# Expert visits of 384 rows, a one-instruction maximum and column sums that move: a change to a filter, routing and feed-forward kernel

## The chip, the core and the metric

The kernel runs on one core of a Trainium2 chip. A core has a matrix engine (TensorE; PE in the profile, with its weight loads as PEld), a vector engine (VectorE, DVE), an activation engine (ScalarE, ACT), a general engine (GpSimd, POOL), and a queue engine that issues most transfers (SyncE, SP). Each engine works through its own list of instructions in order; they wait for one another by semaphores. The metric is the time of one execution on the device in microseconds (us), lower is better.

## The reference

Eight sequences of 3072 tokens with 256 channels pass through three layers. `N` is 8 x 3072 = 24576 tokens.

```
X = rfft(x, axis=1);  y = irfft(X * (filt_r + 1j*filt_i))          # a long convolution, per channel
xn, en = y / |y|, emb / |emb|
logits = xn @ en.T / tau;  e = argmax(logits);  gate = softmax(logits)[e]
y[e] = gate * (relu(y @ w1[e]) @ w2[e])                           # 8 experts, 256 -> 1024 -> 256
h = y @ w_in;  out = (h - tanh(h)) @ w_out                        # 256 -> 2048 -> 256
```

Every matrix product of the last two layers is taken as three products: each operand is split into a high part that the fast matrix format holds exactly and a low rest, and high x high, high x low and low x high are summed.

## The kernel before, in words

The program has three stages that overlap at their ends. In the first, `fft_phase`, the filter is done as matrix products with transfers through device memory between the steps; the router scores each token, and each token's row (256 values, gate and token number) is scattered into a `region` in device memory with one segment of `CAP` rows for each expert, filled from its start.

In the second, class `Moe`, a *visit* takes 256 consecutive rows (`TV`) of one segment through its expert's two layers. There are 103 visits (`NV`): the first nine (`KV`) take rows of the fullest expert among the early batches and run beside the end of the first stage; the other 94 follow a schedule that `moe_schedule` works out on the device, with up to seven spare visits, since each expert's last visit can be part empty. A visit has four steps `b2`, and step by step the generator `visits` (its loop is at the end of the function) issues in this order:

- `up(v, b2)`: 12 matmuls into a PSUM tile `h` (two blocks of 128 hidden features, 6 matmuls each, with 256 rows as columns);
- for visit `v+1`: `split` of one quarter of the expert's weights into high and low (steps 0 and 1: `w1h` on ScalarE, `w1l` on VectorE, L752; steps 2 and 3: `w2h` on ScalarE, `w2l` on GpSimd, L752), and its rows: step 0 scales them by the gate (`ys`, GpSimd L763, and the token numbers `it`, VectorE L766), step 1 transposes them (`yt`, VectorE L771), step 2 splits them (`yh` on ScalarE L778, `yl` on VectorE L779);
- `relu(v, b2)`: `hh` on ScalarE (L801), the rest `hl` on VectorE (L802);
- for visit `v+2`: the transfer of one quarter of the weights (`wload`, skipped on the device where the expert stays the same) and, in step 2, of its rows `y` (`load`, four transfers on SP's queue);
- in step 3 (and in step 1 for the first 7 scheduled visits) one *side step*: a third of the work of converting a 128 x 256 tile of the feed-forward's 64-bit weights (`f64_split`, mostly VectorE);
- `down` of the step two before, 12 matmuls into `o`. After a visit's last `down`, `finish` copies `o` to `x2` and its absolute value to `xa` (ScalarE L823, L825), keeps a running maximum `mx` (VectorE L826), and sends `x2` off.

So TensorE's order at a boundary is `up(v,2) down(v,0) up(v,3) down(v,1) up(v+1,0)`, and the first matmuls of `up(v+1,0)` need `yl` of visit v+1. On VectorE that `yl` stands behind `mx` of visit v-1, which stands behind the last `down` of v-1.

In the third stage, `ff_phase`, 48 tiles of 512 tokens pass through the feed-forward in 16 steps each: 6 matmuls of 512 columns (L961) and 12 of 256 (L1004). Before tile 46 `limit` forms a bound from `mx` and the column sums of |w_in| (`l1`), which decides on the device whether a second, general pass is needed.

Of the kernel before, what the change touches and what calls it, by code (L numbers as in the profile page):

```python
# [27 lines left out]
S = 3072  # L28
E = 8
# [8 lines left out]
TV = 256  # L38
# [79 lines left out]
def fft_phase(tc, K, x, fr, fn, fi, emb, tau, region, base, NB, CAP, moe):  # L118
# [3 lines left out]
    with ExitStack() as es:  # L122
# [288 lines left out]
        for i in range(2 * E):  # L411
            at(31 + i, zeros, i // 2, i % 2 * 128)
# [48 lines left out]
def f64_split(nc, pool, src, hi, lo, n):  # L461

    v = nc.vector
    H, L = src[:, :, 1], src[:, :, 0]
    t = lambda nm, dt: pool.tile([128, n], dt, name=nm)
    a, m, l, f, r = t("cva", I32), t("cvm", I32), t("cvl", I32), t("cvf", F32), t("cvr", F32)
    v.tensor_scalar(a, H, 20, 0x7FF, op0=ALU.logical_shift_right, op1=ALU.bitwise_and)
    v.tensor_scalar(a, a, 896, 0, op0=ALU.subtract, op1=ALU.max)
    v.tensor_scalar(a, a, 255, None, op0=ALU.min)
    v.tensor_scalar(a, a, 23, None, op0=ALU.logical_shift_left)  # L470
    v.tensor_scalar(m, H, 31, 31, op0=ALU.logical_shift_right, op1=ALU.logical_shift_left)
    v.tensor_tensor(a, a, m, op=ALU.bitwise_or)
# [11 lines left out]
    return f  # L484


def ff_weights(tc, cp, cv, w_in, w_out):

    nc = tc.nc
    wih = cp.tile([128, 2, FF], F32R, name="wih")  # L490
    wil = cp.tile([128, 2, FF], F32R, name="wil")
    wo = cp.tile([128, 16, 2, D], F32R, name="wo")
    l1 = cp.tile([128, FF], F32R, name="l1w")
    W = 256

    def load(src):
        s = cv.tile([128, W, 2], I32, name="cvs", bufs=2)
        nc.sync.dma_start(flat(s), src.bitcast(I32))
        return s

    def step_in(s, k, q):
        c = slice(W * q, W * q + W)
        f = yield from f64_split(nc, cv, s, wih[:, k, c], wil[:, k, c], W)
        if k == 0:
            nc.scalar.activation(l1[:, c], f, AF.Abs)
        else:
            nc.scalar.activation(f, f, AF.Abs)
            nc.vector.tensor_tensor(l1[:, c], l1[:, c].bitcast(F32), f, op=ALU.add)

    def steps():  # L510
        todo = [(w_in[128 * k : 128 * k + 128, W * q : W * q + W], step_in, k, q) for k in range(2) for q in range(FF // W)]
        todo += [(w_out[128 * fb : 128 * fb + 128], lambda s, fb: f64_split(nc, cv, s, wo[:, fb, 0], wo[:, fb, 1], D), fb)
                 for fb in range(16)]
        s = load(todo[0][0])
        yield
        for i, (_, f, *args) in enumerate(todo):
            t = load(todo[i + 1][0]) if i + 1 < len(todo) else None
            yield from f(s, *args)
            yield
            s = t  # L520

    return (wih, wil, wo, l1), steps()
# [15 lines left out]
def moe_schedule(tc, cp, cnt, done, numbers, CAP, step):  # L538
# [17 lines left out]
    v.tensor_scalar(t, left, float(TV - 1), None, op0=ALU.add)  # L556
    v.tensor_copy(ti, t)
    v.tensor_scalar(ti, ti, 8, None, op0=ALU.logical_shift_right)
# [59 lines left out]
class Moe:  # L618
# [6 lines left out]
    def __init__(self, tc, gp, region, w1, w2, x2T, ids, mx, N, CAP):  # L625
        self.tc, self.gp, self.region, self.w1, self.w2 = tc, gp, region, w1, w2
        self.x2T, self.ids, self.mx, self.N, self.CAP = x2T, ids, mx, N, CAP
        self.KV = (N - 2 * S) // (8 * TV)
        self.NV = N // TV + 7
# [9 lines left out]
    def choose(self, base, first, dec):  # L639
# [68 lines left out]
    def visits(self):  # L708
# [4 lines left out]
        W, X, H, O, E = {}, {}, {}, {}, {}  # L713

        def load(v):
            y = fp.tile([128, 8, 66], F32, name="y", bufs=3)
            top = 8 * CAP - TV
            r = self.val(self.begin, 0, v, top) if v < KV else self.val(self.sc, v - KV, 0, top)
            rv = region[bass.ds(r, TV)].rearrange("(t j) (i c) -> i j t c", j=32, i=4)
            for i in range(4):  # L720
                d = nc.sync.dma_start(y[32 * i : 32 * i + 32], rv[i])
# [32 lines left out]
        f2 = lambda z: z.rearrange("p k t c -> p (k t c)")  # L754

        def rows(v):

            y, yt = X[v], None
            ys = fp.tile([128, 2, 8, 32], F32, name="ys")
            it = fp.tile([32, 32], I32, name="it", bufs=2)  # L760
            it2 = fp.tile([32, 32], I32, name="it2", bufs=3)
            def scale():
                nc.gpsimd.tensor_tensor(ys.rearrange("p k t c -> p t k c"), y[:, :, :64].rearrange("p t (k c) -> p t k c", k=2),  # L763
                                        y[:, :, 64:65].unsqueeze(3).to_broadcast([128, 8, 2, 32]), op=ALU.mult)
                nc.vector.memset(it, 0)
                nc.vector.tensor_copy(it[:, :8], y[:32, :, 65:66].bitcast(I32).rearrange("p t o -> p (t o)"))  # L766

            def turn():
                nonlocal yt
                yt = ip.tile([128, 2, 8, 32], F32, name="yt")  # L770
                nc.vector.transpose(f2(yt), f2(ys))  # L771
                nc.vector.transpose(it2, it)

            def parts():
                yh = ip.tile([128, 2, TV], F32R, name="yh")
                yl = ip.tile([128, 2, TV], F32R, name="yl")
                X[v] = (yh, yl, it2)
                nc.scalar.activation(flat(yh), f2(yt), AF.Copy)  # L778
                nc.vector.tensor_tensor(flat(yl), f2(yt), flat(yh).bitcast(F32), op=ALU.subtract)  # L779
# [3 lines left out]
        def up(v, b2):  # L783
            w1h, w1l = W[v][:2]
            yh, yl, _ = X[v]
            k = 4 * (v - KV) + b2
            h = self.hp[k // 2 % 2 if k >= 0 else 0].tile([128, 2, TV], F32, name="h")
            for j in range(2):
                c = slice(128 * (2 * b2 + j), 128 * (2 * b2 + j) + 128)
                n = 0  # L790
                for k in range(2):
                    for p, q in ((w1h, yh), (w1h, yl), (w1l, yh)):
                        nc.tensor.matmul(h[:, j], p[:, k, c], q[:, k], start=n == 0, stop=n == 5)  # L793
                        n += 1
            H[v, b2] = h

        def relu(v, b2):
            h = H[v, b2]
            hh = yp.tile([128, 2, TV], F32R, name="hh", bufs=4)
            hl = yp.tile([128, 2, TV], F32R, name="hl", bufs=4)  # L800
            nc.scalar.activation(hh, h, AF.Relu)  # L801
            nc.vector.scalar_tensor_tensor(hl, h, 0.0, hh.bitcast(F32), op0=ALU.max, op1=ALU.subtract)  # L802
            H[v, b2] = (hh, hl)

        def down(v, b2):
            w2h, w2l = W[v][2:]
            hh, hl = H.pop((v, b2))
            if b2 == 0:
                O[v] = self.op[(v - KV + 1) % 2 if v >= KV else 0].tile([128, 2, TV], F32, name="o")
            for j in range(2):  # L810
                fb = 2 * b2 + j
                for d in range(2):
                    c = slice(128 * d, 128 * d + 128)
                    for n, (p, q) in enumerate(((w2h, hh), (w2h, hl), (w2l, hh))):
                        nc.tensor.matmul(O[v][:, d], p[:, fb, c], q[:, j], start=fb == 0 and n == 0 and d == 0,  # L815
                                         stop=fb == 7 and n == 2 and d == 1)
# [244 lines left out]
def build(tc, a, out, NB):  # L1061
# [3 lines left out]
    with ExitStack() as es:  # L1065
# [4 lines left out]
        mx = gp.tile([128, 512], F32, name="mx")  # L1070
        nc.vector.memset(mx, 0.0)
# [3 lines left out]
        moe = Moe(tc, gp, region, a["w1"], a["w2"], x2T, ids, mx, N, CAP)  # L1075
        with tc.manual_schedule():
# [23 lines left out]
            ff_phase(tc, x2T, ids, out, weights, mx, N, todo[1])  # L1100
# [32 lines left out]
```

## Time and profile before

| | us |
|---|---|
| three runs | 4189.06, 4167.3, 4185.1 (median 4185.1) |
| the profiled execution | 4176.74, its span 4174.9 |
| first stage until the first visit | 583.9 |
| nine early visits, until the first scheduled one | 133.0 |
| 94 scheduled visits | 1278.1 |
| feed-forward | 2179.9 |

The stages' bounds are the starts of the first `up` matmul of visit 0, of visit 9, and of the feed-forward. In the profile each engine's busy time counts the union of its instructions; a time in brackets behind an instruction is the idle time of its engine just before it and who ended it. The granted clock is TensorE's, as a share of 2.4 GHz.

### The profile page before, as it was taken

To read this page: it belongs to the slowest core of one execution; us is meant where nothing else is said; L and a number is where in the kernel's file an instruction comes from. 1 tells how busy PE (TensorE), PEld (TensorE's weight loads), DVE (VectorE), ACT (ScalarE), POOL (GpSimd) and SP (SyncE) were. 2 spreads that over 40 slices of the span, in tenths; PEclk is the share of its full clock that TensorE was granted. 3 is DMA by queue.
4 is the path that set the end of the run, shared out by engine and by line. 5 is a ranking of instruction groups with operands and counts; after the bars stand their busy time and mean duration, and the time that the engine had idled before them with its cause. 6 is when DMAs were issued, how large, how long until landed. Compare 5 with 4: busy or idle time off the path is not lost.

```text
span 4174.9 us, 73338 instructions
## 1 busy us (share of the span) xinstructions
PE 3949.5 (95%) x25988; PEld 3562.5 (85%) x25988; DVE 2853.3 (68%) x4459; ACT 2617.5 (63%) x4385; POOL 2199.2 (53%) x1601
## 2 busy tenths in 40 slices
PE   6999889899889998899999999999999999999998
PEld 3666669899889898899999999999999999999987
DVE  4899986989889898898555555555555555555554
ACT  3555544555555555555677777777777777777765
POOL 2466664444444545455455555555555555555555
PEclk8999999999999999999999999999999999999999
DMA  9989753221221222212100000001001000000000
GB/s 270 290 275 287 248 178 88 52 65 49 67 67 48 65 60 55 67 50 60 36 25 27 21 24 29 21 24 29 21 22 30 21 21 28 25 21 28 25 16 17
DMA packets 302863, 297.67 MB, mean 71 GB/s; under 512 B 157457, under 2 KB 245402, under 8 KB 302490
## 3 DMA queue, kind: packets, MB, share of 16 engines
q1 hardware_dynamic: 280666, 238.89, 20.3%
q0 software_dynamic: 18432, 51.14, 3.4%
q8 instruction: 206, 3.38, 0.3%
q10 hardware_dynamic: 3392, 2.90, 0.2%
q14 instruction: 167, 1.37, 0.1%
HBM read 342.33 MB, written 130.72 MB: 113 GB/s over the span
## 4 chain that ended last, share of the span: by engine, by line
PE 51%; DMA 1%; ACT 0%; issue 0%; DVE 0%; POOL 0%; POOLq 0%; ACTq 0%; DVEq 0%
PE po L1004 25%; PE h L961 25%; DMA out<-ob,ix 1%; POOL gl L969 0%; ACT u L976 0%; DVE g L979 0%; DVE s L978 0%; ACT gh L968 0%; ACT s L977 0%; ACT ob L1010 0%; DVE lm L939 0%; POOL out L1013 0%; POOL allmax L944 0%; DVE big L945 0%; DVE big L946 0%
## 5 line engine op out<-in xcount | busy, mean ns | idle before, releaser
L969 POOL TENSOR_TENSOR gl<-g,gh 128x512 fp32r<-128x512 f32 x768 | 997.3, 1299 | 954.6 <-ACT gh L968 946.8
L978 DVE SCALAR_TENSOR_TENSOR s<-s,u 128x512 f32<-128x512 f32 x768 | 534.8, 696 | 936.4 <-ACT s L977 934.7
L1004 PE MATMUL po<-wo,gh 128*128 128x256 f32 x6144 | 1117.1, 280 | 0.0
L1004 PEld LDWEIGHTS po<-wo,gh 128*128 128x128 f32 x6144 | 994.6, 188 | 65.0
L1004 PE MATMUL po<-wo,gl 128*128 128x256 f32 x3072 | 864.4, 281 | 3.9 <-POOL gl L969 3.7
L976 ACT ACTIVATE u<-h 128x512 f32<-128x512 f32 x768 | 458.5, 597 | 591.1 <-PE h L961 591.0
L752 POOL TENSOR_TENSOR w2l<-raw,w2h 128x1024 fp32r<-128x1024 f32 x188 | 501.4, 2686 | 403.4 <-ACT w2h L751 403.3
L961 PE MATMUL h<-xh,wih 128*128 128x512 f32 x1536 | 615.9, 401 | 0.1
L961 PE MATMUL h<-xl,wih 128*128 128x512 f32 x1536 | 605.7, 394 | 0.0
L961 PE MATMUL h<-xh,wil 128*128 128x512 f32 x1536 | 604.4, 393 | 0.0
L979 DVE TENSOR_TENSOR g<-s,h 128x512 f32<-128x512 f32 x768 | 528.4, 688 | 85.9 <-POOL gl L969 3.7
L1004 PEld LDWEIGHTS po<-wo,gl 128*128 128x128 f32 x3072 | 579.2, 189 | 4.3 <-POOL gl L969 4.3
L793 PE MATMUL h<-yl,w1h 128*128 128x256 f32 x1648 | 486.2, 295 | 92.4 <-DVE yl L779 92.4
L977 ACT ACTIVATE s<-u,beta 128x512 f32<-128x512 f32 x768 | 556.1, 724 | 25.2
L815 PE MATMUL o<-hl,w2h 128*128 128x256 f32 x1648 | 482.5, 293 | 27.3 <-DVE hl L802 27.3
L801 ACT ACTIVATE hh<-h 128x512 fp32r<-128x512 f32 x412 | 244.9, 594 | 403.9 <-PE h L793 403.0
L968 ACT ACTIVATE gh<-g 128x512 fp32r<-128x512 f32 x768 | 486.2, 633 | 11.1 <-DVE g L979 6.1
L793 PE MATMUL h<-yh,w1h 128*128 128x256 f32 x1648 | 483.0, 293 | 4.4 <-DVE hl L802 2.8
L793 PE MATMUL h<-yh,w1l 128*128 128x256 f32 x1648 | 482.6, 293 | 2.1 <-DVE w1l L752 2.1
L815 PE MATMUL o<-hh,w2h 128*128 128x256 f32 x1648 | 481.5, 292 | 0.0
L815 PE MATMUL o<-hh,w2l 128*128 128x256 f32 x1648 | 480.0, 291 | 0.0
L793 PEld LDWEIGHTS h<-yl,w1h 128*128 128x128 f32 x1648 | 330.6, 201 | 101.6 <-DVE yl L779 100.7
(198 smaller groups left out, 7131.1 us busy)
## 6 DMA issues: line engine op xcount, KB each, us to landing
raw<-in_w SPq DMA_DIRECT2D x376, 512.0 KB
y<-region SPq DMA_DIRECT2D x412, 66.0 KB
xt<-in_x SPq DMA_DIRECT2D x48, 512.0 KB
z1d<-a SPq DMA_DIRECT2D x96, 256.0 KB
A<-z1d SPq DMA_DIRECT2D x64, 384.0 KB
z3d<-b SPq DMA_DIRECT2D x128, 192.0 KB
bt<-z3d SPq DMA_DIRECT2D x96, 256.0 KB
x2T<-x SPq DMA_DIRECT2D x94, 256.0 KB
```

The costliest lines, as they stand in the source:

```text
L752: eng.tensor_tensor(l, r, h.bitcast(F32), op=ALU.subtract)
L793: nc.tensor.matmul(h[:, j], p[:, k, c], q[:, k], start=n == 0, stop=n == 5)
L801: nc.scalar.activation(hh, h, AF.Relu)
L815: nc.tensor.matmul(O[v][:, d], p[:, fb, c], q[:, j], start=fb == 0 and n == 0 and d == 0, stop=fb == 7 and n == 2 and d == 1)
L961: nc.tensor.matmul(h, a[:, k, c], b[:, k], start=n == 0, stop=n == 5)
L968: nc.scalar.activation(gh, g, AF.Copy)
L969: nc.gpsimd.tensor_tensor(gl, g, gh.bitcast(F32), op=ALU.subtract)
L976: nc.scalar.activation(u, h, AF.Square)
L977: nc.scalar.activation(s, u, AF.Square, bias=beta)
L978: nc.vector.scalar_tensor_tensor(s, s, KAPPA, u, op0=ALU.add, op1=ALU.mult)
L979: nc.vector.tensor_tensor(g, s, h, op=ALU.mult)
L1004: nc.tensor.matmul(po[a // 2][:, a % 2], p[:, a], wo[:, f, q], start=f == 0 and n == 0 and a % 2 == 0, stop=f == 15 and n == 2 and a % 2 == 1)
```

## The change

`TV` becomes 384 for all visits but the first nine, which keep 256 (`TE`). There are then 74 visits, 65 of them scheduled, and the spare ones are of 384 rows too. Each of a visit's two feature blocks gets a PSUM bank of its own (384 of 512 columns), so `h` has four banks as before but two steps fill them instead of four; `o` gets two banks a visit, and two visits alternate over four. The ReLU and the copy to `x2` go in two instructions, one for each bank. `xa` and the running maximum go; one reduction of |x2| on VectorE writes one column of `mx` for each visit. The side step stands in step 1 too for the first 36 scheduled visits. `y` has two buffers instead of three, `hh` and `hl` three instead of four, `yt` one instead of two. The column sums of |w_in| leave the weight conversion and are formed in tile 45 of the feed-forward. The first stage clears 384 rows of each segment instead of 256 (24 transfers instead of 16), and the schedule counts visits by multiplying with 171/512 where it shifted.

```diff
-TV = 256
+TE = 256
+TV = 384
...
-        for i in range(2 * E):
-            at(31 + i, zeros, i // 2, i % 2 * 128)
+        for i in range(TV // 128 * E):
+            at(31 + i, zeros, *divmod(128 * i, TV))
...
-        f = yield from f64_split(nc, cv, s, wih[:, k, c], wil[:, k, c], W)
-        if k == 0:
-            nc.scalar.activation(l1[:, c], f, AF.Abs)
-        else:
-            nc.scalar.activation(f, f, AF.Abs)
-            nc.vector.tensor_tensor(l1[:, c], l1[:, c].bitcast(F32), f, op=ALU.add)
+        yield from f64_split(nc, cv, s, wih[:, k, c], wil[:, k, c], W)
...
-        self.NV = N // TV + 7
+        self.NV = self.KV + (N - self.KV * TE) // TV + 7
+        self.mx = gp.tile([128, self.NV], F32, name="mx")
...
-        self.op.append(self.pool("mo2", 1, space=PSUM))
+        self.op.append(self.pool("mo2", 3, space=PSUM))
...
-            y = fp.tile([128, 8, 66], F32, name="y", bufs=3)
+            y = fp.tile([128, NT, 66], F32, name="y", bufs=2)
...
-            k = 4 * (v - KV) + b2
-            h = self.hp[k // 2 % 2 if k >= 0 else 0].tile([128, 2, TV], F32, name="h")
+            if v < KV:
+                t = self.hp[0].tile([128, 2, TE], F32, name="h")
+                h = [t[:, 0], t[:, 1]]
+                H[v, b2] = [t]
+            else:
+                k = 4 * (v - KV) + b2
+                h = [self.hp[k % 2].tile([128, 512], F32, name="h")[:, :TV] for j in range(2)]
+                H[v, b2] = h
...
-            nc.scalar.activation(hh, h, AF.Relu)
-            nc.vector.scalar_tensor_tensor(hl, h, 0.0, hh.bitcast(F32), op0=ALU.max, op1=ALU.subtract)
+            for j, t in enumerate(h):
+                oh, ol = (hh, hl) if len(h) == 1 else (hh[:, j], hl[:, j])
+                nc.scalar.activation(oh, t, AF.Relu)
+                nc.vector.scalar_tensor_tensor(ol, t, 0.0, oh.bitcast(F32), op0=ALU.max, op1=ALU.subtract)
...
-            nc.scalar.activation(x2, o, AF.Copy)
-            xa = yp.tile([128, 2, TV], F32, name="xa", bufs=1)
-            nc.scalar.activation(xa, o, AF.Abs)
-            nc.vector.tensor_tensor(mx, flat(xa), mx, op=ALU.max)
+            for d in range(2):
+                nc.scalar.activation(x2[:, d], o[d], AF.Copy)
+            nc.vector.tensor_reduce(mx[:, v : v + 1], x2, axis=AX.XY, op=ALU.max, apply_absolute_value=True)
...
+        def column_sums(q):
+
+            c = slice(TM * q, TM * q + TM)
+            a = [cp.tile([128, TM], F32, name=f"abs{k}") for k in range(2)]
+            for k in range(2):
+                nc.scalar.activation(a[k], wih[:, k, c].bitcast(F32), AF.Abs)
+            nc.vector.tensor_tensor(l1[:, c], *a, op=ALU.add)
...
+                if t == NT - 3 and f % 4 == 2:
+                    column_sums(f // 4)
```

The first place is VectorE's order over one visit boundary late in the scheduled visits, where a visit has one side step (the four `cv...` rows are one). Before:

```order
L771 STREAM_TRANSPOSE yt<-ys 128x512
L772 STREAM_TRANSPOSE it_18787<-it 32x32
L802 SCALAR_TENSOR_TENSOR hl<-h,hh 128x512
L826 TENSOR_TENSOR mx<-xa,mx 128x512
L779 TENSOR_TENSOR yl<-yt,yh 128x512
L802 SCALAR_TENSOR_TENSOR hl<-h,hh 128x512 x2
L474 TENSOR_SCALAR cvm<-cvs 128x256
L475 TENSOR_SCALAR cvl<-cvs 128x256
L476 TENSOR_TENSOR cvm<-cvm,cvl 128x256
L477 TENSOR_TENSOR cvf<-cva,cvm 128x256
L752 TENSOR_TENSOR w1l<-raw_5490,w1h 128x1024
```

The same piece of a visit after the change, with its new line numbers:

```order
L778 STREAM_TRANSPOSE yt<-ys 128x768
L779 STREAM_TRANSPOSE it_17096<-it 32x32
L818 SCALAR_TENSOR_TENSOR hl<-h,hh 128x384 x2
L846 TENSOR_REDUCE mx<-x_17163 128x1
L786 TENSOR_TENSOR yl<-yt,yh 128x768
L818 SCALAR_TENSOR_TENSOR hl<-h,hh 128x384 x4
L476 TENSOR_SCALAR cvm<-cvs 128x256
L477 TENSOR_SCALAR cvl<-cvs 128x256
L478 TENSOR_TENSOR cvm<-cvm,cvl 128x256
L479 TENSOR_TENSOR cvf<-cva,cvm 128x256
L757 TENSOR_TENSOR w1l<-raw_5497,w1h 128x1024
```

The order of the pieces is the same; the maximum reads one operand instead of two, and each `hl` is two instructions.

The second place is the same boundary in one of the first 36 scheduled visits after the change, on VectorE:

```order
L778 STREAM_TRANSPOSE yt<-ys 128x768
L779 STREAM_TRANSPOSE it_11692<-it 32x32
L818 SCALAR_TENSOR_TENSOR hl<-h,hh 128x384 x2
L476 TENSOR_SCALAR cvm<-cvs 128x256
L477 TENSOR_SCALAR cvl<-cvs 128x256
L478 TENSOR_TENSOR cvm<-cvm,cvl 128x256
L479 TENSOR_TENSOR cvf<-cva,cvm 128x256
L846 TENSOR_REDUCE mx<-x_11763 128x1
L786 TENSOR_TENSOR yl<-yt,yh 128x768
L818 SCALAR_TENSOR_TENSOR hl<-h,hh 128x384 x4
```

A side step stands there between `hl` of step 1 and the maximum, which the visits of before have only seven times.

## Rows read from the trace of the kernel before

**Rows 1.** The page, busy time and share of the span by engine.
```profile
PE 3949.5 (95%) x25988; PEld 3562.5 (85%) x25988; DVE 2853.3 (68%) x4459; ACT 2617.5 (63%) x4385; POOL 2199.2 (53%) x1601
```

**Rows 2.** Windows: us; PE, PEld, DVE, ACT, POOL busy; granted clock, DMA share, GB/s.
```profile
0.00:583.90 583.90, 499.30 (x2120) 341.33 (x2120) 485.77 (x1037) 282.92 (x717) 326.50 (x302) 0.95 0.85 265
...
716.90:1995.00 1278.10, 1158.37 (x9049) 1148.25 (x9050) 1143.44 (x1579) 732.68 (x1077) 618.79 (x279) 0.94 0.23 59
1995.00:4174.90 2179.90, 2163.71 (x13829) 1952.10 (x13827) 1135.88 (x1595) 1537.91 (x2450) 1189.01 (x961) 1.00 0.08 24
```

**Rows 3.** Who PE waited for in the scheduled visits: us, times, longest.
```profile
PE h L793 <- DVE yl L779: 92.4, 41, 3.8
PE o L815 <- DVE hl L802: 27.3, 9, 5.2
```

**Rows 4.** Timeline of PE: start, us, instruction, idle before and its releaser.
```profile
1501.49 0.28 PE L793 MATMUL h<-yh,w1h 128*128 128x256 f32 x1
...
1507.25 0.28 PE L793 MATMUL h<-yh,w1h 128*128 128x256 f32 x1
...
1518.77 0.28 PE L793 MATMUL h<-yh,w1h 128*128 128x256 f32 x1
1521.42 0.39 PE L793 MATMUL h<-yl,w1h 128*128 128x256 f32 x1 [2.38 <-DVE yl L779]
```

**Rows 5.** Window just behind that wait, columns as in Rows 2.
```profile
1522.60:1525.50 2.90, 2.90 (x16) 2.90 (x15) 2.83 (x5) 1.55 (x2) 1.04 (x1) 0.50 0.00 0
```

**Rows 6.** Timeline of DVE over the same two visits.
```profile
1502.80 0.69 DVE L826 TENSOR_TENSOR mx<-xa,mx 128x512 f32<-128x512 f32 x1 [0.66 <-ACT xa L825]
1504.27 2.48 DVE L779 TENSOR_TENSOR yl<-yt,yh 128x512 fp32r<-128x512 f32 x1 [0.77 <-ACT yh L778]
...
1507.88 1.31 DVE L467 TENSOR_SCALAR cva<-cvs 128x256 int32<-128x256 int32 x1
...
1510.75 1.22 DVE L752 TENSOR_TENSOR w1l<-raw,w1h 128x1024 fp32r<-128x1024 f32 x1
...
1515.84 2.76 DVE L826 TENSOR_TENSOR mx<-xa,mx 128x512 f32<-128x512 f32 x1
1518.53 2.84 DVE L779 TENSOR_TENSOR yl<-yt,yh 128x512 fp32r<-128x512 f32 x1
```

**Rows 7.** Timeline of POOL over the same two visits.
```profile
1503.80 5.23 POOL L752 TENSOR_TENSOR w2l<-raw,w2h 128x1024 fp32r<-128x1024 f32 x2 [7.29 <-ACT w2h L751]
1510.93 1.95 POOL L763 TENSOR_TENSOR ys<-y 128x512 f32<-128x512 f32 x1 [1.90 <-DVE cva L472]
1515.32 5.51 POOL L752 TENSOR_TENSOR w2l<-raw,w2h 128x1024 fp32r<-128x1024 f32 x2 [2.44 <-ACT w2h L751]
```

**Rows 8.** Timeline of PE over one step of the feed-forward.
```profile
2501.15 0.40 PE L961 MATMUL h<-xh,wih 128*128 128x512 f32 x1
...
2502.56 0.40 PE L1004 MATMUL po<-wo,gh 128*128 128x256 f32 x2
...
2503.97 0.40 PE L961 MATMUL h<-xh,wih 128*128 128x512 f32 x1
```

**Rows 9.** Groups by line: shapes, count, busy us, mean ns, idle before.
```profile
L976 ACT ACTIVATE u<-h 128x512 f32<-128x512 f32 x768 | 458.5, 597 | 591.1 <-PE h L961 591.0
L802 DVE SCALAR_TENSOR_TENSOR hl<-h,hh 128x512 fp32r<-128x512 f32 x412 | 268.3, 667 | 38.0 <-ACT hh L801 37.8
L752 DVE TENSOR_TENSOR w1l<-raw,w1h 128x1024 fp32r<-128x1024 f32 x188 | 236.0, 1255 | 5.0 <-ACT w1h L751 4.9
L942 DVE TENSOR_REDUCE bound<-mx 128x1 f32<-128x512 f32 x1 | 0.7, 677 | 0.0
```

**Rows 10.** Timeline of SP's queue, the rows of a later visit.
```profile
1507.04 1.90 SPq L721 DMA_DIRECT2D y<-region  x4
```

**Rows 11.** Timelines of DVE and PE at one change of expert.
```profile
1219.21 0.16 DVE L766 COPY it<-y 32x8 int32<-32x8 int32 x1 [4.73 <-DMA y<-region]
...
1220.02 0.58 PE L815 MATMUL o<-hl,w2h 128*128 128x256 f32 x1 [4.33 <-DVE hl L802]
```

More of the change, by code (lines that the diff above doesn't have):

```diff
@@ L520, in steps @@
             s = t
-    return (wih, wil, wo, l1), steps()
+    return (wih, wil, wo), steps()
 def moe_numbers(tc, cp):
@@ L555, in moe_schedule @@
     v.tensor_tensor(left, cnt, done, op=ALU.subtract)
-    v.tensor_scalar(t, left, float(TV - 1), None, op0=ALU.add)
+    assert TV == 3 * 128 and CAP < 250 * 128
+    v.tensor_scalar(t, left, 127.0, None, op0=ALU.add)
     v.tensor_copy(ti, t)
-    v.tensor_scalar(ti, ti, 8, None, op0=ALU.logical_shift_right)
+    v.tensor_scalar(ti, ti, 7, None, op0=ALU.logical_shift_right)
+    v.tensor_copy(t, ti)
+    v.tensor_scalar(t, t, 2.0, 171.0, op0=ALU.add, op1=ALU.mult)
+    v.tensor_copy(ti, t)
+    v.tensor_scalar(ti, ti, 9, None, op0=ALU.logical_shift_right)
     nv = A("scnv")
@@ L752, in split @@
             eng.tensor_tensor(l, r, h.bitcast(F32), op=ALU.subtract)
-        f2 = lambda z: z.rearrange("p k t c -> p (k t c)")
         def rows(v):
-            y, yt = X[v], None
-            ys = fp.tile([128, 2, 8, 32], F32, name="ys")
+            n = size(v)
+            nt = n // 32
+            y, yt = X[v][:, :nt], None
+            ys = fp.tile([128, 2 * TV], F32, name="ys")[:, : 2 * n]
             it = fp.tile([32, 32], I32, name="it", bufs=2)
@@ L792, in up @@
                     for p, q in ((w1h, yh), (w1h, yl), (w1l, yh)):
[L793 removed]
+                        nc.tensor.matmul(h[j], p[:, k, c], q[:, k], start=n == 0, stop=n == 5)
                         n += 1
[L795 removed]
         def relu(v, b2):
+            n = size(v)
+            hh = yp.tile([128, 2, TV], F32R, name="hh", bufs=3)[:, :, :n]
+            hl = yp.tile([128, 2, TV], F32R, name="hl", bufs=3)[:, :, :n]
             h = H[v, b2]
[L799 to L802 removed]
+            for j, t in enumerate(h):
+                oh, ol = (hh, hl) if len(h) == 1 else (hh[:, j], hl[:, j])
+                nc.scalar.activation(oh, t, AF.Relu)
+                nc.vector.scalar_tensor_tensor(ol, t, 0.0, oh.bitcast(F32), op0=ALU.max, op1=ALU.subtract)
             H[v, b2] = (hh, hl)
@@ L808, in down @@
             if b2 == 0:
-                O[v] = self.op[(v - KV + 1) % 2 if v >= KV else 0].tile([128, 2, TV], F32, name="o")
+                if v < KV:
+                    t = self.op[0].tile([128, 512], F32, name="o")
+                    O[v] = [t[:, :TE], t[:, TE:]]
+                else:
+                    O[v] = [self.op[(2 * (v - KV) + d + 1) % 4 > 0].tile([128, 512], F32, name="o")[:, :TV] for d in range(2)]
             for j in range(2):
@@ L814, in down @@
                     for n, (p, q) in enumerate(((w2h, hh), (w2h, hl), (w2l, hh))):
-                        nc.tensor.matmul(O[v][:, d], p[:, fb, c], q[:, j], start=fb == 0 and n == 0 and d == 0,
-                                         stop=fb == 7 and n == 2 and d == 1)
+                        nc.tensor.matmul(O[v][d], p[:, fb, c], q[:, j], start=fb == 0 and n == 0 and (d == 0 or v >= KV),
+                                         stop=fb == 7 and n == 2 and (d == 1 or v >= KV))
             if b2 == 3:
@@ L914, in ff_phase @@
     nc = tc.nc
-    wih, wil, wo, l1 = weights
+    wih, wil, wo = weights
     NT = N // TM
@@ L1099, in build @@
             moe.go_on(sc, side, ahead)
-            ff_phase(tc, x2T, ids, out, weights, mx, N, todo[1])
+            ff_phase(tc, x2T, ids, out, weights, moe.mx, N, todo[1])
 def arrange(x, filt_r, filt_i, moe_expert_emb, moe_tau, moe_w1, moe_w2, moe2_w_in, moe2_w_out):
```

64 lines of the change are left out of this document (33 added, 31 removed).

## The prediction

> **What bounds the kernel now.** I read the busy shares first [rows 1]: TensorE is busy 95% of the span, so time can only come from its idle stretches, from a slow clock or from fewer columns. The windows by stage say where those are [rows 2]: in the feed-forward TensorE is busy 2163.7 of 2179.9 us at full clock, while the 94 scheduled visits last 1278.1 us with 1158.4 busy, a granted clock of 0.94, and VectorE busy 1143.4, nearly as long as TensorE. That stage is the change's place.
>
> Its floor comes from the timeline of TensorE [rows 4]: from 1501.49 to 1507.25 it does half a visit, 48 matmuls, without a gap: 5.76 us, 0.120 us for 256 columns, 11.52 us a visit, 1082.9 us for 94. So 195.2 us are lost: 119.7 idle (1278.1 - 1158.4) and 75.5 of slowed work. The second follows from the first: behind the wait that ends at 1521.42 a window has granted clock 0.50, that is 1.2 GHz of 2.4 [rows 5]. Each microsecond of waiting has therefore cost 195.2 / 119.7 = 1.63 us.
>
> The waits name two releasers [rows 3]: `yl` (92.4 us, 41 times) and `hl` (27.3 us, 9 times). To see why `yl` is late I laid the timelines of VectorE and GpSimd beside TensorE's, and count from the start of `up(v,2)`: 1501.49 in one visit, 1513.01 (11.52 later) in the next. In both GpSimd starts its two `w2l` of 2.6 us at +2.31 [rows 7]. In the first, `mx` begins at +1.31 and takes 0.69; `yl` then runs beside GpSimd, takes 2.48 and ends at +5.26, when the first `w2l` has ended [rows 6]. TensorE wants it at +5.88. In the second, `mx` begins at +2.83, behind GpSimd's start, and takes 2.76; `yl` follows and takes 2.84, until the second `w2l` has ended. TensorE wanted `yl` at 1518.89 and goes on at 1521.42, 2.53 us late. `mx` was late because VectorE worked from 1506.75 to 1515.84, 9.09 us, without a pause. A visit of 11.52 us is too short for VectorE's list plus its waits for GpSimd.
>
> **The change, part by part.** *Columns.* 94 visits of 256 become 65 of 384: 24960 columns for 24064, 3.7% more. No row shows a matmul of 384 columns. If what 0.120 us holds over 256 / 2.4 = 106.7 ns is a fixed 13.3 ns, it takes 173.3 ns; if all grows with columns, 180.0. The feed-forward's step has 6 matmuls of 512 columns in 1.41 us and 12 of 256 in 1.41 us [rows 8]: there twice the columns take twice the time, 0.235 and 0.1175, so three quarters of 0.235 is 176 ns. I take 178, between that and this stage's own rate: 17.09 us a visit, 1110.9 us for 65, with ends 1081 and 1123. Unlike the waits this part gains nothing; it costs 28 us over 1082.9.
>
> *The wait for `yl`.* `up(v+1,0)` now wants it at 8.54 + 0.18 = +8.72. GpSimd's pair does as much work for a visit as before, so its first `w2l` ends at +2.31 + 2.61 = +4.92 again. VectorE's rate is (1255 - 690) / 512 = 1.10 ns a column, from `w1l` [rows 9] and the free `mx` [rows 6]. `yl` ends at +5.26 + 256 x 1.10 ns = +5.54, 3.2 us early, if the maximum lies ahead of it. From `yl` to the next maximum VectorE had 9.09 us of work; now an `hl` of 384 columns takes 667 - 128 x 1.10 = 526 ns [rows 9], eight of them 1.54 us more than four of 667, and the transposes 0.28 more: 10.91. That ends at +16.45, before the next visit's zero, and the maximum waits for `x2` until +1.31. In the first 36 scheduled visits a second side step is added, 2.87 us (1507.88 to 1510.75, [rows 6]): VectorE is there at +2.23. The maximum itself, a reduction of 768 values, takes 677 + 256 x 1.10 = 0.96 us [rows 9] and ends at +3.19, before +4.92. So `yl` runs in the same gap in every visit, and the waiting of 92.4 us goes. Late next is nothing within 1.73 us; beyond that `yl` falls behind the second `w2l`, ends near +8.8, and with `hl` of step 2 behind it costs TensorE about 0.8 us. I take none.
>
> No row shows a reduction beside GpSimd; beside it `mx` took 0.69 to 2.76. I take 0.96, since the maximum ends before GpSimd's first instruction does in either case. The Trainium skill (SBUF — State Buffer, section SBUF: two separate sides) says that a VectorE instruction with two operands in that memory, or in a two-port mode, and a GpSimd instruction block each other for the whole instruction. The trace agrees for `mx` and `yl`; by that rule the one-operand reduction is not held, which makes the first rival below less likely.
>
> *Two-step depth of `h`.* `up(v+1,0)` needs the banks of `up(v,2)`, so `hl` of step 2. Its first half ends at +5.54 + 0.53 = +6.07, wanted at +8.54: nothing, covered by 2.5 us; without the cover, what is late adds one for one.
>
> *The rows `y`.* Four transfers of half as many bytes again, in two buffers whose readers have ended a visit before. Issued at +5.55 [rows 10], read by GpSimd 3.89 us later [rows 7]; half as long again is +11.4, and VectorE's copy of the token numbers wants them at 5.54 + 4 x 0.526 + 2.87 + 1.16 = +11.7. At a change of expert they come late behind the weights: the copy waited 4.73 us, `hl` behind it, TensorE 4.33 [rows 11]. These are the 27.3 us of [rows 3]. The time from issue to use grows by several microseconds; I keep half, 13.7 x 1.63 = 22 us, with ends 0 and 60.
>
> *Edits with small prices.* The column sums: 8 ScalarE instructions of 0.597 us [rows 9] and 4 of VectorE in the feed-forward, where ScalarE is idle 642 us and VectorE half the time [rows 2]: nothing, at most 8 us without that cover. What they replace leaves the visits, where I count it as nothing. Eight more clearing transfers, 1.08 MB at 265 GB/s in a stage with DMA share 0.85 [rows 2]: 0 to 4 us, I take 2. Four more VectorE instructions on 8 columns in the schedule: at most 4 x 0.68, I take 1. The early visits lose `xa` and `mx` beside TensorE's work: nothing.
>
> *Sum.* 1110.9 + 22 - 1278.1 + 3 = -142. On the profiled run, 4176.7 - 142 = 4034.8; the runs' median lies 8.4 above it, so 4043 us.
>
> **Rivals.** *VectorE stays the bound in the 36 visits with two side steps.* For it: it was the twin of TensorE in [rows 2], and the side steps' own waits for GpSimd may be longer than in my one sample. Against: 1.7 us of room in each visit. If every second of them loses 2.53 x 1.63 = 4.1 us: 18 x 4.1 = 74, 4117 us.
>
> *A matmul has a larger fixed part than I allow*, so that fewer, longer ones pay. If 384 columns took 162.5 ns, 65 visits would last 1014 us and the time would be 3946. Against it stands that both sizes lie above such a line: 120 and 235 ns where it gives 109 and 216. The line is the Trainium skill's (TensorE: Matmul & The Clock Gate, section Back-to-back issue gap): columns / 2.4 plus 2.5 ns. The trace does not agree.
>
> *The rows `y` come late in every visit, and the kernel is slower.* Place: VectorE's copy of token numbers, with `hl` and `w1l` queued behind it, and TensorE behind `hl`. It decides from a landing later than +13.4, some 8 us from issue, twice today's; it outweighs the gain from 142 / 65 = 2.2 us a visit. At the price of a change of expert, 65 x 4.33 x 1.63 = 459: 4502 us. Against it: 3.89 us today, and transfers take a DMA share of only 0.23.
>
> *The gain is eaten at the boundary.* With `h` two steps deep each late `hl` stops TensorE earlier than before; if a visit loses 1.34 us so, 2.2 with the clock, the time stays 4185. It needs VectorE some 4 us behind the timetable above.
>
> **How the numbers follow.** My forecast 0.76, with a range of its own of 3990 to 4095 (from 1081 without waits to 1123 with 60 us of them). The rivals 0.12, 0.04, 0.05 and 0.03. A difference of 0.5%, 21 us, is about what a measurement of this kernel can tell. Faster 0.76 + 0.12 + 0.04 = 0.92, the same 0.03, slower 0.05. The range 3985 to 4115 leaves out the rule's case, the slow one and the tie.
>
> **What would show it.** In the new profile: 65 scheduled visits, most of 16.6 to 17.3 us; matmuls of 384 columns at 173 to 180 ns; almost no wait of TensorE for `yl`; the maximum near 0.96 us; granted clock of the stage above 0.98; waits for `hl` only at changes of expert; feed-forward 2180 us. Wrong would be a stage of over 1200 us, visits that alternate between two lengths, or `it` waiting for `y` in most of them.

## The result and the profile after

The changed kernel took 4030.8 us, median of 4 executions (4024.8 to 4034.2); the kernel before 4181.0 beside it. The ratio is 0.9643, 95% interval 0.9613 to 0.9672. Measured once more on another chip (the last experiment) it is 0.9643 again. The forecast was 4043 us, with a range from 3985 to 4115.

The page of the changed kernel, the row that answers to [rows 1]:

```profile
PE 3904.8 (97%) x23204; PEld 3527.1 (88%) x23204; DVE 2621.8 (65%) x4370; ACT 2514.1 (62%) x4318; POOL 2051.7 (51%) x1514
```

The windows by stage, columns as in [rows 2], with the early visits as second row:

```profile
0.00:590.70 590.70, 501.98 (x2120) 342.19 (x2120) 485.42 (x1037) 282.76 (x717) 327.04 (x302) 0.95 0.84 264
590.70:729.65 138.95, 131.36 (x992) 122.62 (x993) 86.97 (x253) 60.18 (x142) 62.77 (x60) 0.98 0.39 112
729.65:1822.50 1092.85, 1087.21 (x6267) 1085.93 (x6266) 909.67 (x1483) 606.07 (x1004) 476.65 (x193) 1.00 0.27 70
1822.50:4023.00 2200.50, 2184.23 (x13829) 1976.39 (x13828) 1139.70 (x1599) 1565.05 (x2458) 1185.26 (x961) 1.00 0.08 24
```

The scheduled visits went from 1278.1 to 1092.85 us, at full clock, with TensorE idle for 5.6 us instead of 119.7. The other stages became longer: the first by 6.8, the early visits by 5.95 (138.95 - 133.0), the feed-forward by 20.6. Together that is -185.25 + 6.8 + 5.95 + 20.6 = -151.9, the difference of the profiled executions (4176.74 and 4024.83).

Who TensorE waited for in the scheduled visits (us, times, longest); of the two rows of [rows 3] the first has no successor:

```profile
PE h L807 <- DVE hl L818: 5.6, 4, 2.1
```

TensorE's timeline at the quarter points of one late visit:

```profile
1518.81 0.33 PE L807 MATMUL h<-yh,w1h 128*128 128x384 f32 x1
1518.98 0.33 PE L807 MATMUL h<-yl,w1h 128*128 128x384 f32 x1
...
1527.13 0.33 PE L807 MATMUL h<-yh,w1h 128*128 128x384 f32 x1
...
1535.45 0.33 PE L807 MATMUL h<-yh,w1h 128*128 128x384 f32 x1
1535.62 0.33 PE L807 MATMUL h<-yl,w1h 128*128 128x384 f32 x1
```

From 1518.81 to 1535.45 there are 96 matmuls and no gap: 16.64 us, 173.3 ns for 384 columns. 55 of the 65 visits begin 16.64 us before the next.

VectorE from `up(v,2)` (1527.13) of that visit:

```profile
1527.85 0.95 DVE L846 TENSOR_REDUCE mx<-x 128x1 f32<-128x768 f32 x1 [1.52 <-ACT x L845]
1529.54 2.53 DVE L786 TENSOR_TENSOR yl<-yt,yh 128x768 fp32r<-128x768 f32 x1 [0.73 <-ACT yh L785]
1531.99 1.68 DVE L818 SCALAR_TENSOR_TENSOR hl<-h,hh 128x384 fp32r<-128x384 f32 x3
...
1537.18 1.29 DVE L773 COPY it<-y 32x12 int32<-32x12 int32 x1
```

GpSimd beside it, answering to [rows 7]:

```profile
1528.85 5.48 POOL L757 TENSOR_TENSOR w2l<-raw,w2h 128x1024 fp32r<-128x1024 f32 x2 [6.51 <-ACT w2h L756]
1536.30 2.15 POOL L769 TENSOR_TENSOR ys<-y 128x768 f32<-128x768 f32 x1 [1.97 <-DMA y<-region]
```

Counted from 1527.13, the maximum ends at +1.67, before GpSimd begins at +1.72; `yl` ends at +4.94 and is wanted at 1535.62, +8.49: 3.55 us early. The copy `it` finds its rows at +10.05 without waiting.

### The profile page after: what moved, and what is told of

It reads as the page before. It is cut to its first block, busy times and chain, and to the rows that moved or that the text cites. A ratio compares the mean times of both kernels' runs of the same rounds, so it can differ in the third digit from the quotient of the medians.

```text
span 4023.0 us, 65752 instructions
## 1 busy us (share of the span) xinstructions
PE 3904.8 (97%) x23204; PEld 3527.1 (88%) x23204; DVE 2621.8 (65%) x4370; ACT 2514.1 (62%) x4318; POOL 2051.7 (51%) x1514
## 3 DMA queue, kind: packets, MB, share of 16 engines
q1 hardware_dynamic: 275714, 241.83, 21.3%
## 4 chain that ended last, share of the span: by engine, by line
PE 85%; DVE 7%; DMA 4%; issue 2%; POOL 1%; SPq 1%; ACT 1%; POOLq 0%; DVEq 0%; ACTq 0%
PE po L1034 27%; PE h L991 26%; PE h L807 14%; PE o L835 14%; DVE u L261 1%; DVE v L260 1%; DVE v L259 1%; DMA out<-ob,ix 1%; PE z L254 1%; PE z L269 1%; PE z L296 1%; PE L L308 1%; PE z L229 1%; DMA region<-Y,pi 1%; DMA z1d<-a 1%
## 5 line engine op out<-in xcount | busy, mean ns | idle before, releaser
L1034 PE MATMUL po<-wo,gh 128*128 128x256 f32 x6144 | 1143.0, 282 | 0.0
L1006 ACT ACTIVATE u<-h 128x512 f32<-128x512 f32 x768 | 459.0, 598 | 584.1 <-PE h L991 583.9
L757 POOL TENSOR_TENSOR w2l<-raw,w2h 128x1024 fp32r<-128x1024 f32 x130 | 349.9, 2692 | 416.7 <-ACT w2h L756 414.4
L817 ACT ACTIVATE hh<-h 128x384 fp32r<-128x384 f32 (+1 forms) x556 | 269.5, 498 | 458.1 <-PE h L807 443.4
L998 ACT ACTIVATE gh<-g 128x512 fp32r<-128x512 f32 x768 | 485.4, 632 | 11.2 <-PE po L1034 4.9
L807 PE MATMUL h<-yh,w1h 128*128 128x384 f32 (+1 forms) x1184 | 392.4, 331 | 10.7 <-DVE hl L818 7.3
L807 PE MATMUL h<-yh,w1l 128*128 128x384 f32 (+1 forms) x1184 | 389.5, 329 | 2.4 <-DVE w1l L757 2.3
L807 PE MATMUL h<-yl,w1h 128*128 128x384 f32 (+1 forms) x1184 | 389.4, 329 | 0.1
L835 PE MATMUL o<-hh,w2h 128*128 128x384 f32 (+1 forms) x1184 | 388.4, 328 | 0.2 <-ACT x L845 0.2
L835 PE MATMUL o<-hl,w2h 128*128 128x384 f32 (+1 forms) x1184 | 388.2, 328 | 0.0
L835 PE MATMUL o<-hh,w2l 128*128 128x384 f32 (+1 forms) x1184 | 388.1, 328 | 0.0
L991 PEld LDWEIGHTS h<-xh,wil 128*128 128x128 f32 x1536 | 288.5, 188 | 71.0
```

Of the source, the lines that this page charges most:

```text
L757: eng.tensor_tensor(l, r, h.bitcast(F32), op=ALU.subtract)
L807: nc.tensor.matmul(h[j], p[:, k, c], q[:, k], start=n == 0, stop=n == 5)
L817: nc.scalar.activation(oh, t, AF.Relu)
L835: nc.tensor.matmul(O[v][d], p[:, fb, c], q[:, j], start=fb == 0 and n == 0 and (d == 0 or v >= KV), stop=fb == 7 and n == 2 and (d == 1 or ...
L991: nc.tensor.matmul(h, a[:, k, c], b[:, k], start=n == 0, stop=n == 5)
L998: nc.scalar.activation(gh, g, AF.Copy)
```

## The experiments

They ran on four chips; each ratio is against the kernel before on the same chip.

**The maximum alone, with 256 rows** (the kernel before, and):

```diff
-            xa = yp.tile([128, 2, TV], F32, name="xa", bufs=1)
-            nc.scalar.activation(xa, o, AF.Abs)
-            nc.vector.tensor_tensor(mx, flat(xa), mx, op=ALU.max)
+            nc.vector.tensor_reduce(mx[:, v : v + 1], x2, axis=AX.XY, op=ALU.max, apply_absolute_value=True)
```

> The kernel before, with one part of the change: the absolute copy and the running maximum go, one reduction of |x2| takes their place; visits stay at 256 rows. Theory A (the maximum's wait for GpSimd is what makes yl late): the maximum still comes at +2.8 us but ends at +3.5, ahead of the end of GpSimd's first w2l at +4.9, so yl runs in the first gap of every visit and the visits take 11.52 us: scheduled visits 1090 to 1140 us, time 4020 to 4060. Rival B (a visit of 256 rows is too short for VectorE's list, whatever the maximum costs): visits still alternate, scheduled visits over 1200 us, time over 4105.

Measured: 4048.4 us, ratio 0.9704 (0.9675 to 0.9733): theory A, though the stage is 7 us above its range. Its scheduled visits, as a window and by TensorE's waits:

```profile
719.60:1866.30 1146.70, 1106.42 (x9048) 1103.76 (x9049) 1053.23 (x1579) 689.56 (x983) 626.22 (x280) 0.98 0.25 66
```

```profile
PE o L815 <- DVE hl L802: 28.1, 8, 5.7
PE h L793 <- DVE yl L779: 12.1, 4, 3.2
```

The waits for `yl` fell from 92.4 us to 12.1, and 131.4 us of the stage went (in the four profiles with the old maximum and 256 rows the stage takes 1267.3 to 1278.1 us). 79 of the 94 visits last 11.52 us now, so a visit of 256 rows was not too short for VectorE's list as such. Two visits of it show why, VectorE's maxima and GpSimd's work:

```profile
1305.76 0.66 DVE L824 TENSOR_REDUCE mx<-x 128x1 f32<-128x512 f32 x1
1317.71 0.66 DVE L824 TENSOR_REDUCE mx<-x 128x1 f32<-128x512 f32 x1
```

```profile
1305.75 5.24 POOL L752 TENSOR_TENSOR w2l<-raw,w2h 128x1024 fp32r<-128x1024 f32 x2 [2.97 <-ACT w2h L751]
...
1317.27 5.23 POOL L752 TENSOR_TENSOR w2l<-raw,w2h 128x1024 fp32r<-128x1024 f32 x2 [2.53 <-ACT w2h L751]
```

Both maxima run wholly beside GpSimd and take 0.66 us, where the two-operand one took 2.76 [rows 6]. The scheduled visits as a whole say the same, first before, then here: the groups (columns as in [rows 9]), and behind each the shortest, median and longest maximum in ns:

```profile
L826 DVE TENSOR_TENSOR mx<-xa,mx 128x512 f32<-128x512 f32 x94 | 139.1, 1479 | 20.4 <-ACT xa L825 20.4
L826 DVE TENSOR_TENSOR mx<-xa,mx x94: 664/694/2771, 725.6 to 1988.3; 128x512 f32<-128x512 f32 x94
```

```profile
L824 DVE TENSOR_REDUCE mx<-x 128x1 f32<-128x512 f32 x94 | 62.2, 662 | 2.5 <-ACT x L823 2.2
L824 DVE TENSOR_REDUCE mx<-x x94: 656/660/686, 726.2 to 1859.2; 128x1 f32<-128x512 f32 x94
```

Before, 44 of the 94 maxima began while a `w2l` of GpSimd ran, and 43 of them took over 1.2 us; here 70 began so, and none took over 0.69. So the waits did not go because the maximum came at a better time: it is no longer held. The run also drops ScalarE's copy `xa`, for which VectorE had waited 20.4 us in all; that part was not run by itself. The Trainium skill (SBUF — State Buffer, section SBUF: two separate sides) says that a VectorE instruction with two operands in that memory and a GpSimd instruction that reads it block each other for the whole instruction. The trace agrees: 0.66 us with one operand beside GpSimd, 2.76 with two.

**384 rows, but a two-operand maximum** (the changed kernel, and):

```diff
-            nc.vector.tensor_reduce(mx[:, v : v + 1], x2, axis=AX.XY, op=ALU.max, apply_absolute_value=True)
+            m3 = mx.rearrange("p (k n) -> p k n", k=2)[:, :, :n]
+            nc.vector.tensor_tensor(m3, x2, m3, op=ALU.max)
```

> The changed kernel with 384 rows, but the maximum is again an instruction with two operands in SBUF (running maximum of x2, 768 columns; the absolute value is left out). Theory A: at 384 rows the maximum starts at +1.3, before GpSimd's first w2l at +2.3, in visits with one side step, so it is not held there; with two side steps it starts at +2.2 to +2.3 and is held in some visits, then yl goes behind the second w2l and TensorE waits up to 1 us: scheduled visits 1093 to 1125 us. Rival B (length alone decides): 1093 us as in the changed kernel, no waits for yl. If the maximum's form decided alone: over 1150 us.

Measured: 4018.3 us, ratio 0.9630 (0.9602 to 0.9659). Its scheduled visits, and TensorE's waits there:

```profile
737.42:1832.20 1094.78, 1089.65 (x6264) 1087.42 (x6265) 920.12 (x1483) 605.97 (x1003) 470.93 (x192) 1.00 0.27 69
```

```profile
PE h L808 <- DVE hl L819: 7.9, 6, 2.9
```

1094.8 us against 1092.85, and no wait for `yl`, as rival B has it: with 384 rows the form of the maximum hardly matters. Its group in that stage, and its shortest, median and longest:

```profile
L848 DVE TENSOR_TENSOR mx<-x,mx 128x768 f32<-128x768 f32 x64 | 66.4, 1038 | 37.1 <-ACT x L846 36.6
L848 DVE TENSOR_TENSOR mx<-x,mx x65: 693/957/3161, 747.0 to 1820.5; 128x768 f32<-128x768 f32 x64, 128x512 f32<-128x512 f32 x1
```

A mean of 1038 ns for 768 columns, 1479 before for 512: all but three of these maxima begin while no `w2l` runs, most of them before GpSimd starts, and VectorE waits 37.1 us for `x` instead. The three are held, for 1.97 to 3.16 us, which is the hold of theory A, but too seldom to cost more than the 2 us; in the changed kernel three reductions begin beside GpSimd too and take 0.95 us at most. The stage has four corners then: 1278.1 us with neither part, 1146.7 with the reduction, 1094.8 with the rows, 1092.85 with both. Each part takes the waits for `yl` away nearly by itself. The corner with the rows has no `xa` either, and what comes with the rows (more side steps, other buffers) was not taken apart.

**The column sums alone** (the kernel before, with the sums in the feed-forward as in the changed kernel):

```diff
-        f = yield from f64_split(nc, cv, s, wih[:, k, c], wil[:, k, c], W)
...
+        yield from f64_split(nc, cv, s, wih[:, k, c], wil[:, k, c], W)
...
+                if t == NT - 3 and f % 4 == 2:
+                    column_sums(f // 4)
```

> The kernel before, with one part of the change: the column sums of w_in leave the weight conversion and are formed in tile 45 of the feed-forward. Theory A: 16 additions on VectorE and 32 absolute values on ScalarE leave 48 of the 94 visits, which still alternate between 11.5 and 15.4 us: scheduled visits fall by 0 to 15 us from 1278. Rival (VectorE's list is the bound, each of its microseconds counts): 16 x 0.43 us of additions and the waits behind them, more than 20 us. The tiles of the feed-forward move by 4 KB, so its step may change by up to 0.03 us.

Measured: 4175.4 us, ratio 1.0001 (0.9987 to 1.0014). The scheduled visits, and what TensorE waited for:

```profile
724.59:2001.41 1276.82, 1162.07 (x9051) 1151.32 (x9049) 1143.98 (x1571) 729.26 (x1062) 626.31 (x281) 0.94 0.23 59
```

```profile
PE h L787 <- DVE yl L773: 96.1, 43, 3.8
```

1276.8 for 1278.1: the sums were worth nothing in the visits, as forecast. In the changed kernel their tile `l1w`, 2048 columns or 8 KB of each partition, is free during the visits; 384 rows together with `l1w`, `xa` and the old `mx` were not run.

**The feed-forward's tiles moved, nothing else** (the kernel before, so that the feed-forward's working tiles and weights lie where the changed kernel has them):

```diff
+    l1 = cp.tile([128, FF], F32R, name="l1w")
     wih = cp.tile([128, 2, FF], F32R, name="wih")
...
-    l1 = cp.tile([128, FF], F32R, name="l1w")
...
+        cp.tile([128, 2640], F32, name="pad")
```

> The kernel before, its work unchanged; only the places of the feed-forward's tiles are those of the changed kernel (the column sums' tile stands ahead of the weights, an unused tile ahead of the working tiles). Theory P (the places set TensorE's rate there): a step of the feed-forward takes 2.840 us instead of 2.813, feed-forward 2200 us, time 20 us longer, about 4200. Rival Q (something else, such as the engines' relative timing from the start of the stage): 2.813 us and 2180 us.

Measured: 4188.8 us, ratio 1.0036 (1.0021 to 1.0051). Its feed-forward:

```profile
1991.86:4192.90 2201.04, 2185.25 (x13830) 1977.03 (x13828) 1136.70 (x1595) 1562.12 (x2450) 1184.22 (x961) 1.00 0.08 24
```

2201.0 us, the changed kernel's 2200.5, in a kernel that forms no column sums there. So the 20.6 us are not the sums: theory P, although the time grew by 15 us (8.8 to 21.3), not by 20. TensorE's timeline over one step of the changed kernel, beside [rows 8], shows where they sit:

```profile
2500.95 0.40 PE L991 MATMUL h<-xh,wih 128*128 128x512 f32 x1
...
2502.35 0.41 PE L1034 MATMUL po<-wo,gh 128*128 128x256 f32 x2
...
2503.79 0.40 PE L991 MATMUL h<-xh,wih 128*128 128x512 f32 x1
```

The six of 512 columns take 1.40 us, the twelve of 256 take 1.44 (before 1.41 and 1.41): 2.840 us a step for 2.813, in nearly every one of 768 steps, with no wait.

**Other places for the feed-forward's tiles** (the changed kernel; the second is this, the first and third shift the same tiles otherwise):

```diff
+        cp.tile([128, 688], F32, name="pad")
```

> The changed kernel, its work the same; the feed-forward's working tiles stand where they stood before the change, its weights stay 8 KB further. Theory P1 (the working tiles' places set TensorE's rate): a step of 2.813 us, feed-forward 2180 us, time about 4011. Theory P2 (the weights' places): 2.840 us and 4031. If it is how the two lie to each other, neither need come out.

> The changed kernel with an unused tile of 2752 bytes ahead of the feed-forward's working tiles, which puts them and the weights where the run with the two-operand maximum had them. Theory P (places alone): a step of 2.820 us as there, feed-forward 2185 us, time about 4016 instead of 4031. Rival (that run's step came from its maximum): 2.840 us, 4031.

> The changed kernel with the feed-forward's working tiles 8192 bytes further than before the change, as its weights are, so that all tiles lie to each other as before. If the distances between tiles decide: 2.813 us a step, 2180 us, time about 4011. If the addresses themselves do: another step, from 2.80 to 2.84 us.

Measured: 4011.8, 4010.5 and 4012.7 us, ratios 0.9621 (0.9594 to 0.9649), 0.9613 (0.9585 to 0.9641), 0.9618 (0.959 to 0.9645); a step of 2.820 us in all three. The place of the tiles has 15 us to give, and the second run is its theory P. The weights stay 8 KB further in all three, so their place alone does not make the 2.840 (theory P2); that the working tiles go back does not bring 2.813 (theory P1). The third has the distances of before and not its 2.813. Neither theory P1 nor the distances are refuted by that, since a kernel with the very places of before, the one with eight more clears below, reads 2.820 us too.

**The clearing transfers later** (the changed kernel, and):

```diff
-            at(31 + i, zeros, *divmod(128 * i, TV))
+            at(130 + i, zeros, *divmod(128 * i, TV))
```

> The changed kernel with its 24 clearing transfers issued some 100 slots later, when the first stage moves less data. Theory: the eight additional ones delayed the first stage by 9 us at 170 to 195 us; the first visit starts at 584 us or earlier instead of 590.7 and the time falls by 7 to 10 us, to about 4022. Rival (the later start has another cause): 590 us, no change.

Measured: 4033.8 us, ratio 0.9667 (0.9638 to 0.9696), first visit at 604.8 us instead of 590.7. Nothing won, against both theories. The delay only moved: up to 512 us TensorE is at the same matmul within about 1 us of the kernel before, and from 528 us some 9 us behind it.

**Eight more clearing transfers alone, and all 24 spread out** (the kernel before with the first line; the changed kernel with 2752 bytes of padding and the second):

```diff
+            at(31 + 2 * E + i, zeros, i, 0)
...
+            at(31 + 4 * i, zeros, *divmod(128 * i, TV))
```

> The kernel before with eight clearing transfers more, in the same eight places of the first stage where the changed kernel has its third ones (they clear the first 128 rows of each segment once more). Theory C (the eight transfers of 128 rows cost the first stage 7 to 20 us by delaying the transfers beside them): first scheduled visit at 725 to 737 us instead of 717 to 725, time 1.002 to 1.005 of the kernel before. Rival N (the later start of the changed kernel comes from elsewhere, the schedule or the early visits, or is scatter of single profiles): first scheduled visit at 717 to 725 us, ratio 0.999 to 1.001.

> The changed kernel with 2752 bytes left empty ahead of the feed-forward's working tiles (as in the run that reads 2.820 us a step) and with the 24 clearing transfers four places of the first stage apart instead of one. If it is the crowding of the transfers that costs (each delays what is queued beside it for about as long as it lasts), the first visit starts at 584 to 589 us as in the kernel before and the time is 4002 to 4006 us, some 6 to 8 under the version without the spreading. If the transfers cost the same wherever they stand, because the stage is limited by its transfers (DMA share 0.84 there), the first visit starts at 591 to 605 us and the time stays 4008 to 4015 us.

Measured: 4180.0 us, ratio 1.0021 (1.0006 to 1.0037), and 4033.1, ratio 0.9670 (0.9649 to 0.9692). The first is 8.8 us longer (0.0021 x 4168; 2.5 to 15.4), but that is not the clears alone, since its feed-forward took 2185.43 us for 2179.9, a step of 2.820 us for 2.813:

```profile
1999.97:4185.40 2185.43, 2169.22 (x13830) 1958.44 (x13828) 1135.04 (x1595) 1545.87 (x2450) 1185.63 (x961) 1.00 0.08 24
```

What shows the clears is the start of the first visit, 597.4 us. In the four profiles with 16 clears it lies at 583.9 to 588.5, in the eight with 24 at these places at 590.7 to 600.4, means 586.3 and 594.8: theory C. TensorE's timeline shows where it is lost, the same matmuls before:

```profile
174.43 1.03 PE L252 MATMUL z<-A,m 96*128 96x256 f32 x4
...
177.94 1.05 PE L294 MATMUL z<-bt,c 128*128 128x512 f32 x2
```

and with the eight:

```profile
176.67 2.05 PE L252 MATMUL z<-A,m 96*128 96x256 f32 x4 [2.06 <-DMA A<-z1d]
...
187.15 2.05 PE L294 MATMUL z<-bt,c 128*128 128x512 f32 x2 [3.73 <-DMA bt<-z3d]
```

Two waits for loads, 2.06 and 3.73 us, and a slower clock beside them (granted clock 0.80 from 170 to 180 us and 0.67 from 180 to 190; in the kernel before 1.00 in both): from then on the same matmuls start 12 us later than before.

Spreading all 24 made it worse against both theories: 618.3 us. TensorE's longest waits in that first stage:

```profile
PE z L296 <- DMA bt<-z3d: 33.2, 7, 7.1
PE z L269 <- POOL u L262: 30.4, 33, 3.8
PE z L254 <- DMA A<-z1d: 23.7, 9, 10.7
```

The same rows where the 24 stand close together (the last experiment's second kernel):

```profile
PE z L269 <- POOL u L262: 34.7, 35, 3.5
PE z L254 <- DMA A<-z1d: 15.2, 3, 11.3
...
PE z L296 <- DMA bt<-z3d: 6.5, 2, 3.6
```

With the clears among the later loads TensorE waits longer for them, 33.2 us for 6.5 (`bt`) and 23.7 for 15.2 (`A`). So crowding is not what costs. Spreading also moves the transfers, and what each of the two does was not separated.

**The changed kernel and its padded form once more, on one chip** (both unaltered):

> The changed kernel itself, unaltered, on the same chip as the next run. In two pairs of kernels with the same tile places the feed-forward's step differed (2.813 and 2.820 us), so the places alone do not set it. Theory S (the step belongs to the program: places and what else is fixed when it is built): 2.840 us again, feed-forward near 2200 us, and the time 15 to 22 us above the next run. Rival V (the step is drawn anew in every execution or on every chip, and the three readings of 2.840 were chance): a step of 2.813 or 2.820 is as likely here, and the two kernels then differ by less than 8 us.

> The changed kernel with 2752 bytes left empty ahead of the feed-forward's working tiles, unaltered from the run that read 2.820 us a step. Theory S: 2.820 us again, feed-forward near 2186 us, time 4005 to 4015 us. Rival V: 2.813 or 2.840 us as well.

Measured: 4027.7 us, ratio 0.9643 (0.9627 to 0.9659), and 4010.7, ratio 0.9598 (0.9584 to 0.9613). The feed-forward of the one and of the other:

```profile
1824.45:4025.90 2201.45, 2185.40 (x13829) 1977.29 (x13828) 1139.90 (x1599) 1565.18 (x2458) 1185.25 (x961) 1.00 0.08 24
```

```profile
1818.24:4004.10 2185.86, 2170.03 (x13829) 1959.39 (x13828) 1138.54 (x1599) 1548.95 (x2458) 1185.75 (x961) 1.00 0.08 24
```

The steps are 2.840 and 2.820 us again (theory S): the step belongs to the program, not to the execution or the chip. The padded form is 17 us below the changed kernel; no version found is clearly faster.

## Why the prediction was right, and which terms were not

*The waits for `yl`.* Right in mechanism and size: none in the stage. The timetable held where it counted: `yl` was forecast to end at +5.54 and ends at +4.94, since GpSimd begins at +1.72 and not at +2.31. In the visits with two side steps the maximum was forecast to end at +3.19. One of them, counted from 1075.51:

```profile
1075.51 0.33 PE L807 MATMUL h<-yh,w1h 128*128 128x384 f32 x1
```

```profile
1076.48 0.94 DVE L846 TENSOR_REDUCE mx<-x 128x1 f32<-128x768 f32 x1
...
1077.92 2.53 DVE L786 TENSOR_TENSOR yl<-yt,yh 128x768 fp32r<-128x768 f32 x1 [0.49 <-ACT yh L785]
```

It ends at +1.91, so there was more room than I thought. But the prediction credited the pair of edits, and called a visit of 11.52 us too short; the corners above show that each edit alone nearly does it, the reduction without a longer visit.

*Columns.* I took 178 ns; it is 173.3, the end with a fixed 13.3 ns in every matmul. 65 visits are 1081.6 us, 29.3 under the term of 1110.9. What misled me was the feed-forward's ratio of two, where twelve short and six long matmuls do not run at the visits' rate. By the line of the Trainium skill (TensorE: Matmul & The Clock Gate, section Back-to-back issue gap), columns / 2.4 plus 2.5 ns, which the page gives for an isolated matmul, it would have been 162.5; the trace does not agree.

*Changes of expert.* Taken at 22 us. The eight visits longer than 16.64 us at and behind the changes add up to 8.4; with the first visit, which is shorter, and the last it is 11.2 (1092.85 - 1081.6). The copy's wait at one of them is as long as in [rows 11]:

```profile
1020.07 0.16 DVE L773 COPY it<-y 32x12 int32<-32x12 int32 x1 [4.73 <-DMA y<-region]
```

But it comes 12.2 us before TensorE is late, and by 2.10, not 4.33:

```profile
1032.24 0.54 PE L807 MATMUL h<-yh,w1h 128*128 128x384 f32 x1 [2.10 <-DVE hl L818]
```

VectorE has made up for part of the wait by then. It also lost time once more on the way, in a two-operand instruction of the side step beside GpSimd, which takes 0.42 us at 1519.43 in the visit laid out above:

```profile
1027.38 2.61 DVE L474 TENSOR_TENSOR cva<-cva,cvm 128x256 int32<-128x256 int32 x1
```

The slow clock follows as in [rows 5], granted clock 0.56 in the next 2.9 us:

```profile
1033.30:1036.20 2.90, 2.90 (x12) 2.90 (x11) 2.80 (x8) 0.50 (x2) 0.43 (x1) 0.56 0.00 0
```

In the visit laid out the rows `y` came nearly as fast as before: issued at 1532.08, read by GpSimd 4.22 us later, for 3.89, not half as long again.

*Clears and the feed-forward.* These two steps failed. "0 to 4 us, I take 2" for the clears was 6.8 in the profile, and 8.5 by the mean start of the first visit with 24 clears and with 16 (594.8 and 586.3). I priced their bytes, and not the loads `A` and `bt` that come late beside them, nor the slow clock that follows. "Feed-forward 2180 us" was 2200.5: I counted what is added there, and the sums do cost nothing, but freeing 8 KB and adding tiles moved every tile of the stage, and with these places the step takes 2.840 us. The early visits, forecast at nothing, show +5.95; over all profiles they take 133.0 to 136.9 us in the old form and 135.9 to 138.9 in the new (means 135.1 and 137.6), so 2 or 3 us are theirs.

*The sum.* Columns -29.3, changes of expert -10.8, first stage +4.8, early visits with the schedule's 1 us +4.95, feed-forward +20.6: -9.7 together, from -142.2 to -151.9. (By its own terms the sum's 4034.8 us is 4034.5; nothing hangs on it.) So it was luck that the forecast came so near: errors of 40 us and 30 us had opposite signs.

*The rivals.* VectorE as the bound, late rows in every visit and a gain eaten at the banks are refuted by 55 visits of 16.64 us; the column rule by 173.3 ns.

## What to carry to other kernels

When two engines are bound by each other's waits, look for the cheapest edit that breaks the cycle: here one instruction with one operand less gave 131 of the 185 us by itself, and the larger tile would have given 183 without it. Take a matmul's rate for a new size from the stage it will run in; in these visits 256 columns took 120.0 ns and 384 took 173.3, which is columns / 2.4 plus 13.3 ns. After any change of what is allocated, compare the untouched stages too, and price an added transfer by the loads that come late for it, not by its bytes alone.

## What the runs showed of the hardware

The pace of the same matmuls depends on something fixed when the program is built: two programs run again on another chip read 2.840 and 2.820 us a step again. All readings with the changed kernel's places are 2.840 us a step (the kernel, twice; the later clears; the kernel before moved there); all other programs read 2.813 or 2.820. Between these two the places do not decide: in one pair with the same places the added clears go with the slower step (2.813 in the kernel before, 2.820 with eight clears more), in the other the spread clears go with the faster (2.820 in the padded kernel, 2.813 with the clears spread). In the moved kernel and the changed one the loss sits in the matmuls of 256 columns: twelve of them take 1.44 us, against 1.42 in the programs at 2.820 and 1.41 at 2.813. Which property of a place costs 20 ns a step, and what the 7 ns come from, stays open.
